# Windowed attention and Mish MLP: VectorE in written order up to the first product, and attention without GpSimd

## The chip, the core and the metric

The kernel runs on one core of a Trainium2 chip. The core has five engines, each with an instruction queue of its own that it works off in order: TensorE (PE, matrix products; its weight loads are listed apart as PEld), VectorE (DVE), ScalarE (ACT, table functions such as exp and Mish, and copies), GpSimd (POOL) and SyncE (SP, which issues the transfers). They wait for each other through semaphores. TensorE writes to PSUM, eight banks of 128 x 2 KB; VectorE and ScalarE read both PSUM and SBUF. The metric is the time of one execution in device microseconds; lower is better.

## The reference

A causal attention with a window of 128 and a linear bias, for 8 images of 8 heads, 576 positions and 64 columns, then a gated MLP over all 4608 rows of 512 columns with 2048 hidden units:

```python
def _attn_ref(q, k, v):
    scores = scale * np.matmul(q, k.transpose(0, 1, 3, 2))
    ...
    mask = (rel >= 0) & (rel < window)
    scores = np.where(mask, scores + bias[None], -1000000000.0)
    scores = scores - np.max(scores, axis=-1, keepdims=True)
    attn = np.exp(scores)
    attn = attn / (np.sum(attn, axis=-1, keepdims=True) + 1e-09)
    return np.matmul(attn, v).astype(np.float32)

def _moe_ref(x, w_in, w_out):
    h = x @ w_in
    sp = np.where(h > 20.0, h, np.log1p(np.exp(np.minimum(h, 20.0))))
    g = h * np.tanh(sp)
    return (g @ w_out).astype(np.float32)
```

The two weight matrices come in 64-bit floats.

## The kernel before

**Stages.** Per image c (0 to 7, the first 512 positions of each) there are three things: attention, a first product h = x w_in followed by Mish, and a second product by w_out. The 64 last positions of all images are put together as a ninth block. Attention of image 0 stands alone at the head. Attention of image c + 1 is written in between the steps of the second product of image c. Every float32 product is made of three products of high and low parts (float32r): x, the weights and g are each split into a rounded part and the rest.

**Attention.** `attention(b)` lists steps with a due number and sorts them. Heads go in pairs p = 0 to 3. A `unit(b, p, half)` is two blocks of 128 rows for both heads of a pair, so four blocks; `last_unit` does the last 64 rows of the pair. The steps of a unit: `scores` (TensorE into the tile s, two PSUM buffers), `exps` (a fused op on VectorE that scales, adds the bias and takes the row's minimum, then exp on ScalarE with the row's sum into sm), `fold` (adds the two halves of a 256-wide window block, since both use the same keys modulo the mask, and makes 1 / (sum + 1e-9)), `scale` (multiplies by it), `weights` (TensorE transposes, then one VectorE product with the two masks spreads the folded block into its two key blocks), `values` (TensorE, into o) and `split_x`. `last_unit` ends with a VectorE copy of its result into xo and a transfer of xo to memory (xs). xo has two buffers, so the copy of pair 2 uses that of pair 0. Before, `fold` adds on GpSimd (on VectorE in `last_unit`), and `scale` is a GpSimd op for image 0 and a VectorE op for the others.

**Weights.** `load_w` loads a piece of a weight in two halves (tiles wi0 to wi7, wo0 to wo7); all but the last piece, wo7, are issued on SyncE ahead of attention of image 0, and wo7 after the first product of image 0, into the tiles of x. `convert_w` turns a piece's 64-bit words into float32: in each half a ScalarE copy into a PSUM tile (ti or to, which takes the bank po0 or po1, or the bank w for wo7), three VectorE ops on 32-bit words that depend on each other, then a rounded copy on ScalarE and the rest on GpSimd, into si0 to si7 and so0 to so7. `convert_next` converts the next piece in the order wi0 to wi7, wo0 to wo7. Where it is called: at 3.6, 5.6 and 7.6 of image 0's attention (whose first unit starts at 0 and whose eighth at 7), then after each of the eight groups of the first product of image 0 once, from the fourth group on twice. The second product's tiles po0 and po1 take the same banks.

**What sets the order.** All engines' calls go through `InOrder`. TensorE and SyncE are kept in the written order. For the other three a scheduler places each instruction by a timeline that it estimates; it may move VectorE's ops of a conversion past those of attention. Every operation is recorded in line 30, so groups are told apart by their tiles: in the profile's names s, pz, sm, mx, o, x, h, g, gh, gl, po, ti, to, si, so; pz_0l to pz_3l and xo_0l to xo_3l belong to `last_unit` of pairs 0 to 3.

Of the kernel before, what the change touches and what calls it, by code (L numbers as in the profile page):

```python
# [8 lines left out]
F32 = mybir.dt.float32  # L9
# [3 lines left out]
AF = mybir.ActivationFunctionType  # L13
ALU = mybir.AluOpType

WINDOW = 128
P = 128
# [24 lines left out]
def attention_mish_mlp(  # L42
# [33 lines left out]
    at = ctx.enter_context(tc.tile_pool(name="at", bufs=2))  # L76
# [14 lines left out]
    for t in vb:  # L91
# [8 lines left out]
    pe, dve, act, pool, sp = engines = [  # L100
        InOrder(tc, e, e in (nc.tensor, nc.sync))
        for e in (nc.tensor, nc.vector, nc.scalar, nc.gpsimd, nc.sync)
    ]
# [126 lines left out]
    def unit(b, p, half):  # L230
# [6 lines left out]
        st = {}  # L237
        blocks = (0, 1) if half == 0 else (2, 3)
        name = f"{b}_{p}_{half}"
# [32 lines left out]
                )  # L272

        def fold():
            sm, pz = st["sm"], st["pz"]
            two = pz if half else pz[:, 1:4:2]
            pool.tensor_tensor(out=two[:, :, :P], in0=two[:, :, :P], in1=two[:, :, P:], op=ALU.add)
            dve.tensor_scalar(out=sm, in0=sm, scalar1=1e-9, scalar2=None, op0=ALU.add)
            dve.reciprocal(sm, sm)

        def scale():
            (pool if b == 0 else dve).tensor_tensor(
                out=st["pz"][:, :, :P], in0=st["pz"][:, :, :P],
                in1=st["sm"].rearrange("p (c n) -> p c n", n=1).to_broadcast([P, 4, P]), op=ALU.mult,
            )

        def weights():
            pz = st["pz"]
# [44 lines left out]
    def last_unit(b, p):  # L333

        st = {}
        name = f"{b}_{p}l"

        def scores():
            qk, z = qkv[(b, p)]

            st["s"] = qkv[("s", b, p)][:, :, :96]
            for i in range(2):
                pe.matmul(
                    st["s"][:, i, :], lhsT=z, rhs=qk[:, 1, 384 + 96 * i : 480 + 96 * i],
                    start=True, stop=True,
                )

        def exps():
            mx = at.tile([P, 1], F32, tag="mxl", name=f"mx{name}")
            sm = st["sm"] = at.tile([P, 1], F32, tag="sml", name=f"sm{name}")  # L350
            pz = st["pz"] = at.tile([P, 192], F32, tag="pzl", name=f"pz{name}")
            dve.tensor_tensor_reduce(
                out=pz.rearrange("p (a n) -> p a n", a=2), in0=st["s"],
                in1=nl[:, p, :].rearrange("p (a n) -> p a n", a=2), scale=-SCALE, scalar=3.0e38,
                op0=ALU.add, op1=ALU.min, accum_out=mx,
            )
            act.activation(pz, pz, AF.Exp, bias=mx, scale=-1.0, accum_out=sm)

        def fold():
            sm, pz = st["sm"], st["pz"]  # L360
            dve.tensor_scalar(out=sm, in0=sm, scalar1=1e-9, scalar2=None, op0=ALU.add)
            dve.reciprocal(sm, sm)
            dve.tensor_tensor(out=pz[:, :64], in0=pz[:, :64], in1=pz[:, P:], op=ALU.add)
            dve.tensor_scalar(out=pz[:, :P], in0=pz[:, :P], scalar1=sm, scalar2=None, op0=ALU.mult)

        def weights():
            t = st["t"] = ps.tile([P, 512], F32, tag="w", name=f"pt{name}")
            pe.transpose(t[:, :P], st["pz"][:, :P], ident)
            pf = st["pf"] = at.tile([P, 2, 2, 64], F32, tag="pfl", name=f"pf{name}", bufs=1)
            shape = [P, 2, 2, 64]  # L370
            dve.tensor_tensor(
                out=pf, in0=t[:, :P].rearrange("p (u i n) -> p u i n", u=1, i=2).to_broadcast(shape),
                in1=masks[:, :, :64].rearrange("p u (i n) -> p u i n", i=1).to_broadcast(shape),
                op=ALU.mult,
            )

        def values():
            va, vl = qkv[("v", b, p)]
            o = st["t"][:, P : P + LEFT]
            for n, val in enumerate((va[:, 3, :], vl)):  # L380
                for i in range(2):
                    pe.matmul(
                        o[HEAD[i]], lhsT=val[:, HEAD[i]], rhs=st["pf"][:, n, i, :],
                        start=(n == 0), stop=(n == 1), skip_group_check=True,
                    )
            xo = at.tile([P, LEFT], F32, tag="xo", name=f"xo{name}")
            dve.tensor_copy(xo, o)
            sp.dma_start(out=xs[p, :, b * LEFT : (b + 1) * LEFT], in_=xo)

        return [  # L390
            (0.01, scores), (0.5, exps), (0.9, fold), (1.4, weights), (1.995, values),
        ]

    def attention(b):

        steps = []
        for k in range(2 * NP):  # L400
            p, half = divmod(k, 2)
            for u in [unit(b, p, half)] + ([last_unit(b, p)] if half == 0 else []):
                steps += [(k + d, f) for d, f in u]
            if half:
                nxt = (b, p + 2) if p + 2 < NP else (b + 1, p + 2 - NP)
                if 0 < nxt[0] < B:
                    steps.append((k + 0.03, lambda nxt=nxt: load_pair(*nxt)))
                    steps.append((k + 2.01, lambda nxt=nxt: load_v(*nxt)))
        return sorted(steps, key=lambda s: s[0])
# [96 lines left out]
    def convert_next(tags=("po0", "po1")):  # L506
        if conv and conv[0] in raw_w:
            convert_w(*conv.pop(0), tags)

    early = [(k, lambda: convert_next()) for k in (3.6, 5.6, 7.6)]  # L510
    for _, work in sorted(attention(0) + early, key=lambda s: s[0]):
        work()

    for c in range(B + 1):
        for j in range(NJ):
            if c == 0:
                while ("i", j) not in split:
                    convert_next()
            if j == NJ - 1:
                parts(c, 0, 0)  # L520
                parts(c, 0, 1)
            first(c, j)
            if c == 0:
                for _ in range(2 if j > 2 else 1):
                    convert_next()
        if c == 0:
            load_w(*last_w)

        n = 4 * NJ
        steps = []  # L530
        for m in range(2 * NJ):
            for t in range(2):
                steps.append((2 * m + t, lambda m=m, t=t: second(c, *divmod(m, NJ), t)))
            if m >= 2:
                steps.append((2 * m - 4.1, lambda m=m: parts(c, *divmod(m, NJ))))
            if c == 0:
                steps.append((2 * m + 0.5, lambda: convert_next(("w", "w"))))
        if c + 1 < B:
            steps += [((n - 2) / 9.0 * s - 0.2, f) for s, f in attention(c + 1)]
        elif c + 1 == B:  # L540
            steps.append((4.5, last_x))
        for _, work in sorted(steps, key=lambda s: s[0]):
            work()
# [63 lines left out]
```

## Time and profile before

| | us |
|---|---|
| median of three runs | 1056.3 (1055.12 to 1056.61) |
| the profiled execution | 1056.28 |
| its span, first to last instruction | 1054.5 |
| first product of image 0 starts on TensorE | 88.03 |
| second product of image 0 starts | 134.78 |
| first product of image 1 starts | 208.3 |

The profile shows one execution. Section 1 of its page has the busy time of each engine; section 2 cuts the span into 40 slices, with tenths of busy time and the clock that TensorE was granted; the chain of work that ended last is followed back from the end:

```profile
PE 85%; DMA 4%; DVE 4%; issue 3%; POOL 2%; ACT 1%; SPq 0%; POOLq 0%; DVEq 0%
```

In rows of a timeline the columns are start, duration, engine, line, operation, out<-in, sizes and count (of equal instructions merged), and in brackets the idle time before it on its engine and what ended it.

### The profile page before, as it was taken

How to read it: one execution, taken by the hardware profiler on the slowest of the kernel's cores; microseconds unless marked ns; L12 is line 12 of the kernel's file. 1: busy time of each engine (PE TensorE's matmuls, PEld its weight loads, DVE VectorE, ACT ScalarE, POOL GpSimd, SP SyncE). 2: the span in 40 equal slices, each digit the busy share in tenths (PEclk: the TensorE clock that was granted, in tenths of full speed). 3: DMA queues.
4: the chain of work that ended last, by engine and by line, in shares of the span. 5: the costliest groups of instructions: out<-in, count | busy, mean ns of one | idle time of the engine just before them, and what ended most of it. 6: DMA issues, size and time to landing. Idle time of an engine off the chain costs nothing.

```text
span 1054.5 us, 14241 instructions
## 1 busy us (share of the span) xinstructions
PE 998.6 (95%) x5280; PEld 787.4 (75%) x5280; DVE 405.7 (38%) x1166; ACT 391.5 (37%) x926; POOL 309.7 (29%) x270
## 2 busy tenths in 40 slices
PE   4548989999999999999999999999999999999998
PEld 2336867787778877887778777877787778888886
DVE  4998067502760167106630564037501760000000
ACT  2544554323433345215422443235323442222221
POOL 3513754211431044004410342123311441041032
PEclk9567989999999999999999999999999999999999
DMA  8940022200220023002120032002100201000001
GB/s 269 399 159 13 1 66 91 70 1 20 64 71 32 1 62 93 33 1 60 58 68 1 25 93 68 1 24 85 58 21 1 71 25 41 20 21 21 1 1 40
DMA packets 52133, 59.32 MB, mean 56 GB/s; under 512 B 13024, under 2 KB 32608, under 8 KB 52064
## 3 DMA queue, kind: packets, MB, share of 16 engines
q1 hardware_dynamic: 50880, 57.69, 17.1%
q8 instruction: 42, 0.69, 0.3%
q10 hardware_dynamic: 1184, 0.72, 0.2%
q14 instruction: 27, 0.22, 0.1%
HBM read 47.91 MB, written 10.49 MB: 55 GB/s over the span
## 4 chain that ended last, share of the span: by engine, by line
PE 85%; DMA 4%; DVE 4%; issue 3%; POOL 2%; ACT 1%; SPq 0%; POOLq 0%; DVEq 0%
PE po L30 38%; PE h L30 33%; PE s L30 9%; PE o L30 5%; DMA wi<-in_moe_w_in_dram 2%; DMA wo<-in_moe_w_out_dram 1%; DVE pz L30 1%; POOL si L30 1%; DVE ti L30 1%; POOL so L30 1%; DVE to L30 1%; DMA nb<-in_relb_dram 1%; DVE wi L30 0%; SPq L30 0%; DMA first<-in_k_dram 0%
## 5 line engine op out<-in xcount | busy, mean ns | idle before, releaser
L30 PE MATMUL h<-x,si 128*128 128x512 f32 x1728 | 394.9, 390 | 0.0
L30 PEld LDWEIGHTS h<-x,si 128*128 128x128 f32 x1728 | 325.5, 188 | 68.0 <-issue 0.3
L30 PE MATMUL po<-so,gh 128*128 128x512 f32 x1152 | 324.8, 404 | 0.0
L30 POOL TENSOR_TENSOR gl<-g,gh 128x512 fp32r<-128x512 f32 x144 | 193.6, 1344 | 376.5 <-ACT gh L30 347.0
L30 PEld LDWEIGHTS po<-so,gh 128*128 128x128 f32 x1152 | 207.5, 189 | 48.6 <-ACT x L30 7.0
L30 DVE CUSTOM_DVE_ANT_0 pz<-s,nb 128x256 f32<-128x256 f32 (+1 forms) x256 | 84.6, 386 | 345.6 <-PE s L30 336.0
L30 PE MATMUL po<-so,gl 128*128 128x512 f32 x576 | 178.7, 391 | 0.0
L30 ACT ACTIVATE g<-h 128x1024 f32<-128x1024 f32 x72 | 74.0, 1028 | 268.8 <-PE h L30 268.8
L30 ACT ACTIVATE pz<-pz,mx 128x256 f32<-128x256 f32 (+1 forms) x256 | 120.3, 471 | 118.0 <-DVE mx L30 117.9
L30 POOL TENSOR_TENSOR pz<-pz 128x256 f32<-128x256 f32 x64 | 64.8, 1013 | 314.9 <-PE po L30 174.0
L30 ACT ACTIVATE gh<-g 128x512 fp32r<-128x512 f32 x144 | 90.6, 629 | 116.6 <-PE po L30 112.4
L30 PEld LDWEIGHTS po<-so,gl 128*128 128x128 f32 x576 | 108.6, 188 | 24.2
L30 DVE TENSOR_TENSOR pz<-s,masks 128x1024 f32<-128x1024 f32 x64 | 78.2, 1222 | 29.2 <-PE s L30 29.2
L30 DVE TENSOR_TENSOR pz<-pz,sm 128x512 f32<-128x512 f32 x56 | 61.9, 1106 | 11.0 <-POOL pz L30 8.9
L30 DVE COPY ob<-po 128x512 f32<-128x512 f32 x18 | 12.4, 692 | 124.9 <-PE po L30 124.9
L30 PE MATMUL s<-qk 64*128 64x128 f32 (+1 forms) x448 | 57.7, 376 | 0.0
L30 PE MATMUL o<-pz,va 128*64 128x128 f32 (+1 forms) x560 | 54.9, 325 | 0.0
L30 PEld LDWEIGHTS o<-pz,va 128*64 128x64 f32 x560 | 33.3, 136 | 27.8 <-issue 10.2
L30 ACT ACTIVATE x<-o 128x512 fp32r<-128x512 f32 x32 | 19.1, 598 | 83.8 <-PE o L30 83.8
L30 PE MATMUL o<-pz,first 128*64 128x128 f32 (+1 forms) x80 | 14.1, 517 | 36.0 <-DVE pz L30 36.0
L30 PE MATMUL s<-ident,pz 128*128 128x128 f32 x256 | 41.1, 286 | 7.4 <-POOL pz L30 4.3
L30 ACT ACTIVATION_READ_ACCUMULATOR pz<-pz,mx 128x1 f32 x256 | 47.8, 187 | 0.0
(114 smaller groups left out, 556.9 us busy)
## 6 DMA issues: line engine op xcount, KB each, us to landing
wi<-in_moe_w_in_dram SPq DMA_DIRECT2D x16, 512.0 KB, 10.4
wo<-in_moe_w_out_dram SPq DMA_DIRECT2D x16, 512.0 KB, 10.8
out_dram<-ob SPq DMA_DIRECT2D x32, 256.0 KB, 2.0
qk<-in_q_dram SPq DMA_DIRECT2D x28, 288.0 KB, 3.7
qk<-in_k_dram SPq DMA_DIRECT2D x28, 288.0 KB, 3.7
va<-in_v_dram SPq DMA_DIRECT2D x28, 256.0 KB, 2.9
first<-in_q_dram SPq DMA_DIRECT2D x4, 288.0 KB, 3.9
first<-in_k_dram SPq DMA_DIRECT2D x4, 288.0 KB, 4.4
```

Source lines behind the costliest of these rows:

```text
L30: ins = method(*args, **kwargs)
```

## The change

VectorE's wrapper is switched to the written order (`dve.fixed = True`) from the head of image 0's attention until the load of wo7 behind its first product. Of the three conversions in that attention the one at 7.6 stays, and each group of the first product is now followed by two. In attention of all images, GpSimd's addition goes: for the blocks that are 256 wide, one fused VectorE op per block adds the two halves and multiplies by the reciprocal (its minimum output `un` is not read); the two blocks that are 128 wide (in units with half 0) are scaled on ScalarE, and the addition of 1e-9 moves from VectorE to ScalarE.

```diff
         def fold():
+            sm = st["sm"]
+            act.activation(sm, sm, AF.Copy, bias=1e-9)
+            dve.reciprocal(sm, sm)
+
+        def scale():
+
             sm, pz = st["sm"], st["pz"]
-            two = pz if half else pz[:, 1:4:2]
-            pool.tensor_tensor(out=two[:, :, :P], in0=two[:, :, :P], in1=two[:, :, P:], op=ALU.add)
-            dve.tensor_scalar(out=sm, in0=sm, scalar1=1e-9, scalar2=None, op0=ALU.add)
-            dve.reciprocal(sm, sm)
-
-        def scale():
-            (pool if b == 0 else dve).tensor_tensor(
-                out=st["pz"][:, :, :P], in0=st["pz"][:, :, :P],
-                in1=st["sm"].rearrange("p (c n) -> p c n", n=1).to_broadcast([P, 4, P]), op=ALU.mult,
-            )
+            unread = at.tile([P, 4], F32, tag="un", name=f"un{name}")
+            for c in range(4):
+                if half or c % 2:
+                    dve.tensor_tensor_reduce(
+                        out=pz[:, c, :P], in0=pz[:, c, :P], in1=pz[:, c, P:], scale=sm[:, c : c + 1],
+                        scalar=3.0e38, op0=ALU.add, op1=ALU.min, accum_out=unread[:, c : c + 1],
+                    )
+                else:
+                    act.activation(pz[:, c, :P], pz[:, c, :P], AF.Copy, scale=sm[:, c : c + 1])
...
         def fold():
             sm, pz = st["sm"], st["pz"]
-            dve.tensor_scalar(out=sm, in0=sm, scalar1=1e-9, scalar2=None, op0=ALU.add)
+            act.activation(sm, sm, AF.Copy, bias=1e-9)
             dve.reciprocal(sm, sm)
-            dve.tensor_tensor(out=pz[:, :64], in0=pz[:, :64], in1=pz[:, P:], op=ALU.add)
-            dve.tensor_scalar(out=pz[:, :P], in0=pz[:, :P], scalar1=sm, scalar2=None, op0=ALU.mult)
+            un = at.tile([P, 1], F32, tag="unl", name=f"un{name}")
+            dve.tensor_tensor_reduce(
+                out=pz[:, :64], in0=pz[:, :64], in1=pz[:, P:], scale=sm, scalar=3.0e38,
+                op0=ALU.add, op1=ALU.min, accum_out=un,
+            )
+            act.activation(pz[:, 64:P], pz[:, 64:P], AF.Copy, scale=sm)
...
-    early = [(k, lambda: convert_next()) for k in (3.6, 5.6, 7.6)]
-    for _, work in sorted(attention(0) + early, key=lambda s: s[0]):
+
+    dve.fixed = True
+    for _, work in sorted(attention(0) + [(7.6, convert_next)], key=lambda s: s[0]):
         work()
...
             if c == 0:
-                for _ in range(2 if j > 2 else 1):
+                for _ in range(2):
                     convert_next()
         if c == 0:
             load_w(*last_w)
+            dve.fixed = False
```

What this does to the engines' queues is seen at three places. In the names the first figure is the image (or the weight's number for ti, to, si, so, wi, wo), and the last one a buffer. The first place is VectorE around the copy of xo for pair 2 of image 0. Before:

```order
L30 COPY xo0_2l_458<-pt0_2l_426 128x64
L30 TENSOR_SCALAR ti7_1_761<-ti7_1_761 128x512
L30 TENSOR_SCALAR to0_0_796<-to0_0_796 128x512
L30 SCALAR_TENSOR_TENSOR ti7_1_761<-wi7_158,ti7_1_761 128x512
L30 ISA pz0_3_0_470,mx0_3_0_468<-s0_3_0_461,nb_76 128x128
```

After:

```order
L30 RECIPROCAL sm0_2_1_409<-sm0_2_1_409 128x4
L30 ISA pz0_2_1_410,un0_2_1_435<-pz0_2_1_410,sm0_2_1_409 128x128
L30 COPY xo0_2l_449<-pt0_2l_429 128x64
L30 ISA pz0_3_0_461,mx0_3_0_459<-s0_3_0_452,nb_76 128x128
L30 TENSOR_TENSOR pz0_2_1_410<-s0_2_1_400,masks_91 128x2x4x128
```

Before, words of wi7 and wo0 stand around the copy (those of wi0 to wi6 are ahead of it); after, no conversion is ahead of it, and pair 3's first softmax op follows directly. The second place is ScalarE around the first Mish of image 0 (g, with the table load ahead of it). Before:

```order
L30 ACTIVATE to4_1_916<-wo4_173 128x512
L30 ACTIVATE to5_0_924<-wo5_176 128x512
L30 ACT_TABLE_LOAD
L30 ACTIVATE g0_0_612<-h0_0_587 128x1024
L30 ACTIVATE si3_614<-wi3_146 128x512 x2
L30 ACTIVATE si4_655<-wi4_149 128x512 x2
```

After:

```order
L30 ACTIVATE x0_3_582<-o0_3_556 128x512
L30 ACTIVATE ti2_0_628<-wi2_143 128x512
L30 ACTIVATE ti2_1_635<-wi2_143 128x512
L30 ACT_TABLE_LOAD
L30 ACTIVATE g0_0_610<-h0_0_585 128x1024
L30 ACTIVATE si1_612<-wi1_140 128x512 x2
L30 ACTIVATE gh0_0_0_981<-g0_0_610 128x512
L30 ACTIVATE si2_627<-wi2_143 128x512
```

The rounded copies behind the first Mish were those of pieces 3 and 4; now they are those of pieces 1 and 2. In the second form the instruction that waits for h (a wait of its own, not shown as a row) stands ahead of the table load; before it is the Mish itself that waits. The third place is ScalarE at the end of the first product of image 0. Before:

```order
L30 ACTIVATE so3_866<-wo3_170 128x512 x2
L30 ACTIVATE g0_3_906<-h0_6_881 128x1024
L30 ACTIVATE so4_908<-wo4_173 128x512 x2
L30 ACTIVATE so5_923<-wo5_176 128x512 x2
L30 ACTIVATE g0_3_906<-h0_7_946 128x1024
L30 ACTIVATE to7_0_1017<-wo7_0_987 128x512
L30 ACT_TABLE_LOAD
```

After:

```order
L30 ACTIVATE to4_0_910<-wo4_173 128x512
L30 ACTIVATE to7_0_1045<-wo7_0_1015 128x512
L30 ACTIVATE so3_894<-wo3_170 128x512
L30 ACTIVATE to4_1_917<-wo4_173 128x512
L30 ACTIVATE so4_909<-wo4_173 128x512
L30 ACTIVATE g0_3_949<-h0_6_924 128x1024
L30 ACTIVATE to5_0_952<-wo5_176 128x512
L30 ACTIVATE g0_3_949<-h0_7_989 128x1024
L30 ACTIVATE to7_1_1052<-wo7_1_1016 128x512
```

The copy of wo7's first half, which waits for that piece's load, stood behind the last Mish; now it stands ahead of the last two, and the copies of wo4 and wo5 stand between them.

More of the change, by code (lines that the diff above doesn't have):

```diff
@@ L274, in fold @@
         def fold():
-            sm, pz = st["sm"], st["pz"]
-            two = pz if half else pz[:, 1:4:2]
-            pool.tensor_tensor(out=two[:, :, :P], in0=two[:, :, :P], in1=two[:, :, P:], op=ALU.add)
-            dve.tensor_scalar(out=sm, in0=sm, scalar1=1e-9, scalar2=None, op0=ALU.add)
+            sm = st["sm"]
+            act.activation(sm, sm, AF.Copy, bias=1e-9)
             dve.reciprocal(sm, sm)
         def scale():
-            (pool if b == 0 else dve).tensor_tensor(
-                out=st["pz"][:, :, :P], in0=st["pz"][:, :, :P],
-                in1=st["sm"].rearrange("p (c n) -> p c n", n=1).to_broadcast([P, 4, P]), op=ALU.mult,
-            )
+            sm, pz = st["sm"], st["pz"]
+            unread = at.tile([P, 4], F32, tag="un", name=f"un{name}")
[7 more added lines that the diff above has]
+                    act.activation(pz[:, c, :P], pz[:, c, :P], AF.Copy, scale=sm[:, c : c + 1])
         def weights():
```

## The prediction

> **What bounds the kernel now.** First the page: busy times and the clock in its 40 slices; then the span cut into five stages at events of the timeline.
>
> ```profile
> PE 998.6 (95%) x5280; PEld 787.4 (75%) x5280; DVE 405.7 (38%) x1166; ACT 391.5 (37%) x926; POOL 309.7 (29%) x270
> PEclk9567989999999999999999999999999999999999
> ```
>
> TensorE is busy 95% of the span, and after the first six slices its clock is granted in full. The stages (columns: stretch, its length, then busy time and count of each engine, granted clock, DMA share, GB/s):
>
> ```profile
> 0.00:88.03 88.03, 40.96 (x229) 27.42 (x229) 72.20 (x194) 38.90 (x107) 27.69 (x44) 0.71 0.73 252
> 88.03:133.45 45.42, 45.42 (x194) 37.20 (x192) 13.08 (x22) 25.79 (x39) 29.54 (x24) 0.96 0.00 1
> 133.45:153.60 20.15, 15.88 (x68) 11.65 (x68) 14.72 (x36) 11.99 (x30) 13.66 (x11) 0.83 0.25 84
> 153.60:208.30 54.70, 54.70 (x354) 41.83 (x354) 35.09 (x105) 22.13 (x69) 19.59 (x16) 1.00 0.23 69
> 208.30:1054.50 846.20, 841.64 (x4441) 669.33 (x4439) 270.56 (x812) 292.70 (x682) 219.23 (x176) 1.00 0.12 37
> ```
>
> Until 88.03 it is VectorE (72.20 of 88.03) that works on the first image's attention and on the weights' words. The first product of image 0 then runs without a gap to 133.45. Between 133.45 and 153.60 TensorE lacks 4.27 us; from 153.60, the first attention-times-values of image 1, it never waits (its busy time fills the stretches up to a few records missing from the trace). So only the head of the kernel can give or lose time. TensorE's order of work is the same after the change, so the result is set by when it reaches that same instruction.
>
> **The change, step 1: when the first product starts.** VectorE now does the attention in written order, with one weight converted in it instead of what the scheduler slipped in. That takes more than 30 us of conversion off VectorE before the product, so attention runs faster at first; no transfer is moved. But written order also makes the copy of xo for pair 2 stand ahead of pair 3's work, and that copy reuses the buffer of pair 0 (two buffers), which a store to memory must have read:
>
> ```profile
> 9.60 0.29 DVE L30 CUSTOM_DVE_ANT_0 pz<-s,nb 128x128 f32<-128x128 f32 x1 [9.60 <-DMA first<-in_k_dram]
> 9.82 0.29 DVE L30 CUSTOM_DVE_ANT_0 pz<-s,nb 128x128 f32<-128x128 f32 x1
> 16.37 1.55 PE L30 MATMUL o<-pz,first 128*64 128x256 f32 x8 [1.26 <-DVE pz L30]
> 51.99 0.33 SPq L30 DMA_DIRECT2D xs<-xo_0l  x1
> xs<-xo_0l SPq DMA_DIRECT2D x1, 32.0 KB, 9.1
> 64.60 0.21 DVE L30 COPY xo_2l<-pt_2l 128x64 f32<-128x64 f32 x1
> ```
>
> The store is issued at 51.99, behind the last weight load on SyncE, and lands 9.1 us later, at 61.1, since seven weight loads are queued before it. SyncE's order and those loads don't change, so it lands at 61.1 again. Before, the copy ran at 64.60 and waited for nothing. After, VectorE gets there in the forties: in the one unit that no weight disturbed it read the first scores at 9.60 and the values product ran at 16.37, 6.8 us later, and five units and a half at 6.5 to 6.8 make 36 on top of 9.6. So VectorE stands for about 14 us with everything of pair 3 queued behind the copy. What is left from 61.1, by the rows of the same work before:
>
> ```profile
> 67.05 0.42 DVE L30 CUSTOM_DVE_ANT_0 pz<-s,nb 128x256 f32<-128x256 f32 x1
> 67.39 0.42 DVE L30 CUSTOM_DVE_ANT_0 pz<-s,nb 128x256 f32<-128x256 f32 x1
> 68.61 1.22 DVE L30 TENSOR_TENSOR pz<-s,masks 128x1024 f32<-128x1024 f32 x1
> 69.88 1.98 PE L30 MATMUL o<-pz,first 128*64 128x128 f32 x12 [4.87 <-DVE pz L30]
> 71.79 2.08 PE L30 MATMUL s<-first 64*128 64x256 f32 x8
> 83.02 1.11 PE L30 MATMUL s<-ident,pz 128*128 128x128 f32 x4 [2.09 <-POOL pz L30]
> 99.28 1.30 DVE L30 TENSOR_SCALAR to<-to 128x512 uint32<-128x512 uint32 x2 [3.80 <-ACT to L30]
> 103.18 0.70 DVE L30 TENSOR_SCALAR to<-to 128x512 uint32<-128x512 uint32 x1 [0.23 <-ACT to L30]
> 103.91 0.70 DVE L30 SCALAR_TENSOR_TENSOR to<-wo,to 128x512 uint32<-128x512 uint32 x1
> 104.64 0.69 DVE L30 SCALAR_TENSOR_TENSOR wo<-wo,to 128x512 uint32<-128x512 uint32 x1
> 88.03 45.49 PE L30 MATMUL h<-x,si 128*128 128x512 f32 x192
> 208.46 43.52 PE h L30 x192
> ```
>
> Scores of 3_0 and the mask of 2_1 to 63.5 (two softmax ops 0.21 apart, two 0.34 apart, then the mask, 1.1); values and the next scores on TensorE, 1.9 + 2.1, to 67.8; four softmax ops at 0.34, a mask and the small one, to 70.7; then the one early weight. Its three ops in a half depend on each other and start 0.73 apart where nothing is put between them (103.18 to 104.64), while two that don't depend take 1.30 together, 0.6 apart. So a half takes 0.73 + 0.73 + 0.6, about 2.05, and a weight 4.1, to 74.8, and the unit's reciprocal stands behind it. Reciprocal and four fused ops (0.21 apart, as the 128-wide softmax op) to 75.7; then transposes, mask and values, which from 83.02 to 88.03 took 5.0 with about 1 of other VectorE work between: **the first product starts at 79.7**, 8.3 earlier than 88.03. ScalarE's new small ops, of 1 to 128 columns, have no row: they cost more than nothing and less than the 0.58 of a 512-wide copy below (2.31 for four); I take 0.2 to 0.3. At five of eight units they lie in the 14 us of standing and cost nothing; for the rest both ends together move the sum by under 0.5. GpSimd's additions and scalings go, for units before the copy in the same shadow.
>
> **Step 2: the first product itself.** Before, weights 0 to 2 were ready at its start; after, weight 0 alone is. Weight 1's copy on ScalarE stands behind the table load and the first Mish (the rows of the change above), and the Mish's wait for TensorE now stands ahead of the table load, which before ran while the product did.
>
> ```profile
> 92.35 1.28 ACT L30 ACT_TABLE_LOAD   x1
> 95.48 1.03 ACT L30 ACTIVATE g<-h 128x1024 f32<-128x1024 f32 x1 [1.85 <-PE h L30]
> 96.40 2.31 ACT L30 ACTIVATE si<-wi 128x512 fp32r<-128x512 f32 x4
> 97.13 5.14 POOL L30 TENSOR_TENSOR si<-wi,si 128x512 fp32r<-128x512 f32 x4 [14.16 <-ACT si L30]
> ```
>
> A group of 24 products takes 43.52 / 8 = 5.44 at full clock; the first product of before lost 45.49 - 43.52 = 2.0 to the half clock at its start, and I give group 0 the 1.1 that falls into it, so it ends at 86.3. Then 1.28 table, 0.92 Mish, 0.6 copy: TensorE waits 2.8 us, gets the high part at 89.1, and the low halves from GpSimd at 90.4 and 91.6 (5.14 for four). With the clock back at half, group 1 ends near 97.8, where an undisturbed one would end at 91.7: **6.1 lost**. Later groups need 5.44 each and a weight comes every 4.1 to 4.5, so they follow without gaps: the product ends at 97.8 + 6 x 5.44 = 130.5, only 3 us ahead of 133.45.
>
> **Step 3: after it.** The second product's first tile takes the same PSUM bank (po0) that the conversions use. Before, VectorE was through with them at 105.3 (104.64 + 0.69). After, 14 weights are left when the last split ends, two 512-wide ops of 0.6 behind the last values: 81.1. To the last half in that bank stand 27 halves at 2.03, 54.8; six ops of the last weight at 0.6, 3.6; softmax of image 1's first unit with its reciprocals and fused ops, 2.4; and waits for ScalarE, which is in order too. Those: behind the first Mish 2.0, behind the second one, late with group 1, 2.6, and 1.6 in which ScalarE stands for the last weight's load, with about 1.3 in small ones. That load's wait now stands ahead of copies and of two Mish:
>
> ```profile
> 136.38 0.62 ACT L30 ACTIVATE to<-wo 128x512 f32<-128x512 f32 x1 [1.65 <-DMA wo<-in_moe_w_out_dram]
> 132.94 0.95 SPq L30 DMA_DIRECT2D wo<-in_moe_w_out_dram  x2
> 146.26 1.09 PE L30 MATMUL s<-ident,pz 128*128 128x128 f32 x4 [3.12 <-DVE pz L30]
> 148.50 0.45 PE L30 MATMUL pt_0l<-ident,pz_0l 128*128 128x128 f32 x1 [1.14 <-DVE wo L30]
> 134.78 1.18 PE L30 MATMUL po<-so,gh 128*128 128x512 f32 x4
> ```
>
> The sum is 149.4, less some 0.9 where two weights interleave: **the second product starts at 148.5**, against 134.78. On the way TensorE stands twice: for the Mish of the last groups, some 8 us to 138.3, before it may write image 1's scores, then 7.5 for the bank. From the second product's start to the first values of image 1 before took 18.82, of which 4.26 waits (the two quoted) and about 2.6 half clock (0.83 granted over 20.15 is 6.9 at half, some 5.2 of them busy), so 11.9 of work; after, with 1.7 of half clock, 13.6: 162.1 instead of 153.60. **So 8.5 us later.**
>
> **What may block the fused ops.** They read two operands from SBUF. The nearest rows, the addition of 64 columns alone and under a GpSimd op:
>
> ```profile
> 29.66 0.21 DVE L30 TENSOR_TENSOR pz_1l<-pz_1l 128x64 f32<-128x64 f32 x1
> 142.36 0.74 POOL L30 TENSOR_TENSOR pz<-pz 128x256 f32<-128x256 f32 x1
> 142.59 0.59 DVE L30 TENSOR_TENSOR pz_0l<-pz_0l 128x64 f32<-128x64 f32 x1
> ```
>
> At 142.59 it ended just behind GpSimd's op, 0.38 late. A fused op may be like it, or free like the softmax op, which reads PSUM and one SBUF tile. Two places have GpSimd busy on the path, the scale of 3_1 at 75 and that of image 1's first unit at 147: 0 to 2 x 1.3 us, perhaps 4 with the clock windows missed. I take one, 1.3, as the addition is the nearer row. The Trainium skill, page "SBUF — State Buffer", section "Who interferes with whom", says that a VectorE instruction with two SBUF inputs contends with a GpSimd instruction that reads SBUF; by that rule both are blocked and the time would be 1069, without it 1065. The row at 142.59 agrees for the addition; no row has the fused op.
>
> **Steady part.** From image 1 on an attention unit has slack:
>
> ```profile
> 165.82 1.29 POOL L30 TENSOR_TENSOR pz<-pz 128x512 f32<-128x512 f32 x1 [3.41 <-ACT pz L30]
> 167.58 1.34 DVE L30 TENSOR_TENSOR pz<-pz,sm 128x512 f32<-128x512 f32 x1
> 172.91 0.60 PE L30 MATMUL s<-ident,pz 128*128 128x128 f32 x4
> ```
>
> The last exponential ends before 165.82 and the transposes come at 172.91. After: 0.3 + 0.1 + four fused ops, 0.85, or four times 1.3 if each is blocked: 171.4 at worst, still in time. I cost the seven later images at nothing; without that cover each unit would add what it is late.
>
> **The sum.** The profiled execution took 1056.28 (span 1054.5 and 1.78 around it), the median is 1056.3. 1056.3 + 8.5 + 1.3 = **1066**.
>
> **Rivals.** (a) VectorE's words keep ahead, faster than before: ops at 0.6 throughout, as in the interleaved pieces, and no wait for ScalarE give 84 x 0.6 = 50.4 us from 81.1, so the bank is free at 131.5, about when the first product ends. Then only steps 1 and 2 count, and the 4.3 us of waits before go too: 1056.3 - 8.3 + 6.1 - 4.3 = 1050. It decides at one point, whether weight words end before TensorE is through group 7. Against it: dependent ops do start 0.73 apart in the one stretch without neighbours. 0.07. (b) The copy doesn't stand, because the store lands soon after its issue: the product starts some 8 us earlier, the words too, and the bank is free at 141: about 1057, no change. Against it is the 9.1. With other partial reliefs 0.08. (c) Blocking bites at both places and at later units: 1069 to 1074, 0.15. (d) My forecast, 1060 to 1069: 0.70.
>
> A difference of 0.2%, 2.1 us, is about what a measurement of this kernel can tell from no change. Faster by more: (a), 0.07. Within: (b), 0.08. Slower: 0.85. The range that holds 8 in 10 runs from 1059 to 1072: its low end has half of step 3's waits gone, its high end both blocks and one more clock window at half.
>
> **What would show it.** Right: VectorE idle from about 46 to 61.1 ahead of the xo copy of pair 2; first product at 79 to 81; a gap of 3 us before its second group with the table load behind the first; first second-product at 148 to 152, waiting for VectorE; the first values of image 1 at 161 to 166; no TensorE idle later. Wrong: no idle ahead of the copy; a second product before 140; TensorE gaps that repeat in each image.

## The result, and the profile after

The changed kernel takes 1067.47 us (median of 4 runs, 1065.71 to 1069.18) beside 1056.23 us for the kernel before (4 runs, 1055.12 to 1056.61): a ratio of 1.0108, 95% interval 1.009 to 1.0126. Timed once more in a later comparison it was 1067.89 beside 1055.91, 1.0118 (1.0103 to 1.0134). It is slower by 11 to 12 us, about 1.1%.

| us | before | after |
|---|---|---|
| the profiled execution | 1056.28 | 1065.71 |
| its span | 1054.5 | 1064.0 |
| first product of image 0, start to end | 88.03 to 133.45 | 80.25 to 130.49 |
| second product of image 0 starts | 134.78 | 149.93 |
| first values of image 1 | 153.60 | 163.06 |
| from there to the end of the span | 900.9 | 900.94 |

The last row says where to look: behind the first values of image 1 the two executions are alike to 0.1 us, so the 9.5 us by which the spans differ arise ahead of them. The medians lie 11.2 us apart: the profiled execution of the changed kernel is the shortest of its four, and e9 below shows where 1.3 us of the rest arise. First the page of the changed kernel, busy times and the clock in 40 slices:

```profile
PE 997.9 (94%) x5280; PEld 786.3 (74%) x5280; DVE 401.8 (38%) x1398; ACT 431.6 (41%) x1118; POOL 233.4 (22%) x198
PEclk9659969999999999999999999999999999999999
```

TensorE's busy time is that of before. GpSimd lost 76 us of work, and ScalarE gained 40; by the last row of the table above, that changes nothing behind the first values of image 1. Then the stages (stretch, its length, busy time and count of PE, PEld, DVE, ACT and POOL, granted clock, DMA share, GB/s):

```profile
0.00:80.25 80.25, 39.09 (x229) 25.88 (x229) 39.34 (x165) 29.77 (x106) 6.51 (x24) 0.73 0.79 276
80.25:130.49 50.24, 46.60 (x194) 37.42 (x192) 43.38 (x65) 32.86 (x52) 29.77 (x23) 0.95 0.00 1
130.49:149.93 19.44, 2.75 (x13) 1.86 (x13) 18.01 (x43) 14.24 (x32) 7.76 (x6) 0.56 0.15 54
149.93:163.06 13.13, 13.13 (x56) 10.04 (x56) 6.06 (x15) 6.63 (x16) 8.71 (x7) 0.88 0.16 49
```

VectorE's work of the head moved and did not shrink: up to the first product it has 39 us instead of 72, during that product 43 instead of 13. In the third stretch, from the end of the first product to the start of the second, TensorE works 2.75 of 19.44 us. Before, that stretch took 1.33 us (133.45 to 134.78), so it is 18.1 longer; 3.0 of them come back because the first product ends earlier, and 5.7 because the stretch behind it takes 13.13 us instead of 18.82. What VectorE does in it, and why it is late, is in its timeline (the row with SPq is SyncE's issue of the store, and the row under it the time from this issue to its landing):

```profile
46.01 0.08 DVE L30 DVE_READ_ACCUMULATOR2_ANT un<- 128x1 f32 x1
51.34 0.33 SPq L30 DMA_DIRECT2D xs<-xo_0l  x1
xs<-xo_0l SPq DMA_DIRECT2D x1, 32.0 KB, 9.1
60.49 0.23 DVE L30 COPY xo_2l<-pt_2l 128x64 f32<-128x64 f32 x1 [14.40 <-DMA xs<-xo_0l]
74.77 0.35 DVE L30 CUSTOM_DVE_ANT_0 pz<-pz,sm 128x128 f32<-128x128 f32 x1
75.04 1.38 DVE L30 CUSTOM_DVE_ANT_0 pz<-pz,sm 128x128 f32<-128x128 f32 x1
147.44 1.35 DVE L30 CUSTOM_DVE_ANT_0 pz<-pz,sm 128x128 f32<-128x128 f32 x1
149.20 0.68 DVE L30 SCALAR_TENSOR_TENSOR wo<-wo,to 128x512 uint32<-128x512 uint32 x1
```

VectorE stands 14.40 us ahead of the copy of pair 2, released by the store of xo for pair 0. That store is issued at 51.34 and lands 9.1 us later, at 60.4; over all eight images the same store takes 2.2 us in the median, and between 40 and 54 us, with the weight loads in flight, the DMA queues move 410 GB/s. Later two fused ops take 1.38 and 1.35 us where the one beside them takes 0.35. The op at 149.20 is the last word in bank po0; it ends at 149.88. TensorE's timeline has the other half, with ScalarE's table load between the first two groups:

```profile
80.25 6.32 PE L30 MATMUL h<-x,si 128*128 128x512 f32 x24
86.64 1.28 ACT L30 ACT_TABLE_LOAD   x1 [0.17 <-PE h L30]
89.55 0.73 PE L30 MATMUL h<-x,si 128*128 128x512 f32 x2 [2.99 <-ACT si L30]
138.29 1.65 PE L30 MATMUL s<-qk 64*128 64x128 f32 x8 [7.80 <-ACT g L30]
149.93 2.07 PE L30 MATMUL po<-so,gh 128*128 128x512 f32 x4 [8.89 <-DVE wo L30]
163.06 0.87 PE L30 MATMUL o<-pz,va 128*64 128x256 f32 x8
```

It waits 2.99 us for weight 1, 7.80 us for the Mish of the last groups, and 8.89 us for VectorE's words, until 0.05 us after the op above ended.

### The profile page after: what moved, and what is told of

It reads as the page before. It is cut to its first block, busy times and chain, and to the rows that moved or that the text cites. A ratio compares the mean times of both kernels' runs of the same rounds, so it can differ in the third digit from the quotient of the medians.

```text
span 1064.0 us, 14440 instructions
## 1 busy us (share of the span) xinstructions
PE 997.9 (94%) x5280; PEld 786.3 (74%) x5280; DVE 401.8 (38%) x1398; ACT 431.6 (41%) x1118; POOL 233.4 (22%) x198
## 4 chain that ended last, share of the span: by engine, by line
PE 90%; DMA 5%; DVE 3%; issue 1%; SPq 1%; ACT 0%; POOL 0%; POOLq 0%; DVEq 0%
PE po L30 38%; PE h L30 36%; PE s L30 9%; PE o L30 5%; DMA wi<-in_moe_w_in_dram 2%; DMA wo<-in_moe_w_out_dram 1%; DVE pz L30 1%; DMA xs<-xo_0l 1%; SPq L30 1%; DVE to L30 1%; DMA nb<-in_relb_dram 1%; DMA first<-in_k_dram 0%; DVE ti L30 0%; DVE wo L30 0%; PE pt_1l L30 0%
## 5 line engine op out<-in xcount | busy, mean ns | idle before, releaser
L30 POOL TENSOR_TENSOR gl<-g,gh 128x512 fp32r<-128x512 f32 x144 | 188.1, 1307 | 711.8 <-ACT gh L30 684.0
L30 DVE CUSTOM_DVE_ANT_0 pz<-pz,sm 128x128 f32<-128x128 f32 x192 | 87.2, 500 | 1.3
L30 PEld LDWEIGHTS s<-qk 64*128 64x128 f32 x448 | 34.3, 188 | 19.1 <-ACT g L30 8.2
L30 PEld LDWEIGHTS s<-ident,pz 128*128 128x128 f32 x256 | 33.1, 146 | 18.6 <-issue 5.9
```

Source lines behind the costliest of these rows:

```text
L30: ins = method(*args, **kwargs)
```

## The experiments

Every run was timed beside the kernel before; ratios are to it. Each edit is against the changed kernel, except where the text says otherwise.

| run | us | ratio (95%) |
|---|---|---|
| changed kernel, second time (e9) | 1067.89 | 1.0118 (1.0103 to 1.0134) |
| e1 four xo buffers | 1051.68 | 0.9967 (0.9956 to 0.9979) |
| e2 attention edit alone | 1054.62 | 0.9991 (0.9982 to 0.9999) |
| e3 written order alone | 1064.73 | 1.0085 (1.0073 to 1.0097) |
| e10 written order alone, four xo buffers | 1050.91 | 0.9954 (0.9941 to 0.9967) |
| e11 kernel before, four xo buffers | 1055.79 | 1.0000 (0.9991 to 1.0009) |
| e4 other banks for the words | 1065.07 | 1.0092 (1.0079 to 1.0105) |
| e5 three weights in the standing | 1048.25 | 0.9931 (0.9919 to 0.9943) |
| e7 two GpSimd reads away | 1065.54 | 1.0094 (1.0081 to 1.0107) |
| e8 table loaded early | 1067.51 | 1.0102 (1.0089 to 1.0115) |
| e6 combined | 1040.68 | 0.9864 (0.9851 to 0.9877) |
| e12 combined, attention as before | 1041.48 | 0.9870 (0.9852 to 0.9887) |

**The changed kernel again (e9).** No edit.

> The changed kernel itself, timed once more beside the two below, since runs of these kernels spread by 3 to 5 us. All theories: 1065 to 1069, ratio to the kernel before 1.009 to 1.013.

It came out as in the first comparison, so the other runs can be set against either. Its profiled execution took 1067.05 us, 1.34 more than that of the first comparison, and VectorE's timeline says why:

```profile
61.76 0.23 DVE L30 COPY xo_2l<-pt_2l 128x64 f32<-128x64 f32 x1 [15.60 <-DMA xs<-xo_0l]
```

SyncE issued the store at 52.59 instead of 51.34, the copy ran 1.27 us later, and everything behind it is shifted by the same: the first product starts at 81.50, the second at 151.20, the first values of image 1 at 164.40. So the difference between these two executions is the landing of this store, and profiles of kernels that stand for it are best compared counted from the copy.

**The standing ahead of the xo copy (e1).**

```diff
-            xo = at.tile([P, LEFT], F32, tag="xo", name=f"xo{name}")
+            xo = at.tile([P, LEFT], F32, tag="xo", name=f"xo{name}", bufs=4)
```

> The changed kernel with four buffers for xo instead of two, so that the copy of pair 2's last unit waits for no store. Nothing else is changed. Theory (the 14.4 us for which VectorE stands ahead of that copy are the price of the written order, and all that follows moves with it): the copy runs at about 47 instead of 60.5, the first product starts at 68 to 70 instead of 80.25, the second at 136 to 139 instead of 149.93, and the time is 1053 to 1056, 12 to 14 us less than the changed kernel and as fast as or faster than the kernel before. First rival (the prediction's case b): the earlier start is partly eaten by the words, which still have to be converted; the product starts 8 us earlier and the time is near 1057. Second rival (the words of the 14 remaining weights alone set the second product, whenever the first one starts): the product starts at 69, but the second stays at 147 to 150 and the time at 1065 to 1067.

The time falls by 15 us, from slower than before to faster than before. VectorE's timeline in this run:

```profile
47.06 0.23 DVE L30 COPY xo_2l<-pt_2l 128x64 f32<-128x64 f32 x1 [0.45 <-PE pt_2l L30]
```

And TensorE's:

```profile
69.34 6.84 PE L30 MATMUL h<-x,si 128*128 128x512 f32 x24
79.19 1.22 PE L30 MATMUL h<-x,si 128*128 128x512 f32 x2 [3.00 <-ACT si L30]
137.66 2.07 PE L30 MATMUL po<-so,gh 128*128 128x512 f32 x4 [9.09 <-DVE wo L30]
151.92 0.87 PE L30 MATMUL o<-pz,va 128*64 128x256 f32 x8
```

The copy runs 13.4 us earlier, the first product 10.9, the second 12.3, the first values of image 1 11.1. The waits ahead of the second group and of the second product, 3.00 and 9.09, are as they were, and that for the Mish of the last groups is 5.09 instead of 7.80: the whole chain moved. So the standing is what makes the change a loss, and neither rival of this run holds. The profiled execution of this run took 1054.56, as the theory had it; it was the longest of ten (1049.61 to 1054.56), and the median lies 1.3 below the range expected.

**The two parts apart (e2, e3).** e2 puts the new `fold` and `scale` into the kernel before; e3 takes them out of the changed kernel.

> The kernel before with the attention edit alone: GpSimd's addition and scaling replaced by the fused ops and ScalarE's scaled copies; the scheduler still orders VectorE and all three early conversions stay. Theory (the edit shortens the chain of each unit of image 0, since GpSimd's addition of 1.3 us and its scaling go, and costs nothing in the later images because the units there have slack): the first product starts 2 to 3 us earlier than 88.03, the time is 1052 to 1054. Rival (the fused ops are blocked by GpSimd in many places and the two small ops on ScalarE lengthen the chain): the first product starts at 88 to 90 and the time is 1056 to 1059.

> The changed kernel with attention as it was before: only VectorE's written order up to the first product and the moved conversions are left. Theory (the written order is what costs; it does so by the standing ahead of the xo copy and by the weights that are not ready): VectorE idle to about 61 ahead of the copy, first product at 80 to 81, second at 147 to 150, time 1062 to 1066. Rival (the two parts add up: whatever the attention edit alone brings against the kernel before is what this kernel lacks against the changed one): the time is the changed kernel's 1067.5 plus what the attention edit saves alone, so 1070 to 1072 if that saves 3 to 4 us. Second rival (attention costs the loss): near 1056.

The attention edit alone is a small gain, 0.9991: less than the theory's 2 to 4 us, but no loss, so its rival falls as well. In its profile TensorE's rows read:

```profile
85.96 45.78 PE L30 MATMUL h<-x,si 128*128 128x512 f32 x192
146.73 0.45 PE L30 MATMUL pt_0l<-ident,pz_0l 128*128 128x128 f32 x1 [2.93 <-DVE wo L30]
151.97 0.87 PE L30 MATMUL o<-pz,va 128*64 128x256 f32 x8
```

The first product starts 2.1 us earlier, of which 1.6 reach image 1; a wait for the last weight's words, 1.14 us before, is now 2.93. The written order alone is the loss, 1.0085, and it shows the same standing, in VectorE's timeline of e3:

```profile
61.24 0.23 DVE L30 COPY xo_2l<-pt_2l 128x64 f32<-128x64 f32 x1 [16.34 <-DMA xs<-xo_0l]
```

The two ratios give 1.0076 when multiplied; both together measured 1.0108 and 1.0118. So the parts do not seem to just add up: on top of the written order the attention edit costs some 3 us (the interval of e3 overlaps that of the first comparison and is clear of that of e9). The first rival of e3 (1070 to 1072) had the sign of that the wrong way. Two candidates for these 3 us are the blocked fused ops and the table load (e7, e8 below): with the old attention, TensorE's gap ahead of the second group was 1.68 us and not 2.99. The profiled executions do not place them further: e3's was the longest of its five and the changed kernel's the shortest of its four, and the first values of image 1 come at 163.23 and 163.06. Counted from the xo copy, the second product starts 4.0 us earlier in e3, but the first values of image 1 only 0.6.

**Where the buffers bind (e10, e11).** The edit of e1, once in e3 and once in the kernel before.

> Only the written order and the moved conversions, attention as before, and four buffers for xo. Theory (without the standing the written order is a gain by itself, and the attention edit adds nothing to it because its two blocked fused ops and the table load behind the wait cost about what GpSimd's addition did): first product at 68 to 70, time 1048 to 1052, the same as with the attention edit (1051.7) or up to 3 us less. Rival (the attention edit is worth here what it was worth alone): 1052.5 to 1055, 1 to 3 us more than with it.

> The kernel before with four buffers for xo and nothing else. Theory (the store's landing binds only where the written order puts the copy early; in the kernel before, the copy of pair 2 ran at 64.60, after the landing at 61.1): no change, within 0.2% of the kernel before, first product at 87 to 89. Rival (the two buffers held the scheduler's order back too, unseen): the first product starts 3 us or more earlier and the time falls to 1050 to 1053.

In the kernel before, four buffers do nothing (ratio 1.0000): its copy ran after the store had landed in any case, and the rival falls. With the written order they take 14 us off e3. The attention edit, which costs some 3 us with two buffers, makes no measurable difference with four (0.9967 with it, 0.9954 without, intervals that overlap); whether its cost depends on the buffers at all is not shown, since 0.13% and 0.23 to 0.33% are too close for these intervals. The written order with its moved conversions, once the copy does not stand, is 0.5% faster than the kernel before.

**The bank of the words (e4).**

```diff
                 for _ in range(2):
-                    convert_next()
+                    convert_next(("w", "o"))
```

> The changed kernel with the conversions behind the groups of the first product put into the PSUM banks w and o instead of po0 and po1, so that no conversion holds a bank of the second product. Theory as the prediction put it (the held bank po0 is what delays the second product, and so image 1): the 8.89 us wait for VectorE ahead of the second product is gone, it starts at 139 to 142 instead of 149.93, the first values of image 1 come 8 to 10 us earlier and the time is 1057 to 1060. Rival (the bank only carries the wait; VectorE's words stand ahead of image 1's reciprocals and fused ops, so the queue is the bound): the second product starts at 139 to 142, but TensorE then waits for VectorE 5 to 8 us ahead of image 1's transposes or values, and the time is 1063 to 1066, only 2 to 4 us less than the changed kernel.

TensorE's timeline in this run:

```profile
139.98 1.64 PE L30 MATMUL po<-so,gh 128*128 128x512 f32 x4
157.59 0.45 PE L30 MATMUL pt_0l<-ident,pz_0l 128*128 128x128 f32 x1 [7.33 <-DVE wo L30]
162.37 0.87 PE L30 MATMUL o<-pz,va 128*64 128x256 f32 x8
```

And VectorE's:

```profile
151.00 0.08 DVE L30 DVE_READ_ACCUMULATOR2_ANT un_0l<- 128x1 f32 x1
156.75 0.69 DVE L30 SCALAR_TENSOR_TENSOR wo<-wo,to 128x512 uint32<-128x512 uint32 x1
```

The second product starts right behind image 1's first scores, 9.95 us earlier: the bank was the cause of the 8.89. But the time comes down by only 2 to 3 us (the intervals of the changed kernel and of this run still overlap), as the rival had it. TensorE now waits 7.33 us at the transposes of image 1's last unit. What they read was ready at 151.08 (the fused op behind `un_0l`); they go only when the word at 156.75 has ended, at 157.44. Those transposes write to bank w, which the last weight's words hold in both kernels. So the wait moved from one held bank to the next, and the rival's time is right but its reason is not shown: it named the order of VectorE's queue. Whether that order alone would hold image 1 back, were no bank held, wasn't tried.

**Words in the standing (e5).**

```diff
-    for _, work in sorted(attention(0) + [(7.6, convert_next)], key=lambda s: s[0]):
+    for _, work in sorted(attention(0) + [(5.99, lambda: convert_next())] * 3, key=lambda s: s[0]):
```

> The changed kernel (two xo buffers) with three weights converted directly ahead of pair 2's last values and xo copy, instead of one at the end of image 0's attention. VectorE so has 3 x 4.1 = 12.3 us of words to do in the 14.4 us for which it stood. Theory (the standing is free time on VectorE that only lacks work written ahead of it; what the words of later weights cost is time after the first product): the copy still runs at 60 to 61, the first product starts at 76, four us earlier than 80.25 as no words are left behind the copy, the 3 us gap ahead of its second group is gone, the second product starts 17 to 20 us earlier (130 to 133), and the time is 1047 to 1051. Rival (the words held the attention up elsewhere, or ScalarE's and GpSimd's share of them lands on the chain of pair 3): the first product stays at 80 or later, and the time is 1058 to 1064: the gap and one weight are saved, no more.

VectorE's timeline around the copy:

```profile
46.32 0.69 DVE L30 TENSOR_SCALAR ti<-ti 128x512 uint32<-128x512 uint32 x1
58.09 0.69 DVE L30 SCALAR_TENSOR_TENSOR wi<-wi,ti 128x512 uint32<-128x512 uint32 x1
61.60 0.23 DVE L30 COPY xo_2l<-pt_2l 128x64 f32<-128x64 f32 x1 [2.82 <-DMA xs<-xo_0l]
```

And TensorE's:

```profile
75.17 32.93 PE L30 MATMUL h<-x,si 128*128 128x512 f32 x144
111.00 11.17 PE L30 MATMUL h<-x,si 128*128 128x512 f32 x48 [2.90 <-ACT g L30]
127.76 1.66 PE L30 MATMUL s<-qk 64*128 64x128 f32 x8 [5.59 <-ACT g L30]
130.22 2.05 PE L30 MATMUL po<-so,gh 128*128 128x512 f32 x4
143.26 0.87 PE L30 MATMUL o<-pz,va 128*64 128x256 f32 x8
```

The copy waits for the same store and runs 1.1 us later than it did, as the store was issued 1.1 later (52.42), but 18 word ops (46.32 to 58.78) fill the time before it. Six groups run without a gap from 75.17, and the second product waits for no word; what is left are two waits for a Mish, 2.90 and 5.59. That is 19 us better than the changed kernel, with the buffers unchanged and the copy no earlier, and 3 to 4 us better than e1, which took the wait away. So the 14.4 us were lost not because VectorE waited, but because nothing was written ahead of the wait.

**The blocked fused ops (e7).** The second halves of weight 0 of w_in and weight 5 of w_out get a low part of zero.

```diff
-            pool.tensor_tensor(out=low, in0=val, in1=up.bitcast(F32), op=ALU.subtract)
+            if (kind, j, a) in (("i", 0, 1), ("o", 5, 1)):
+                pool.memset(low.bitcast(F32), 0.0)
+            else:
+                pool.tensor_tensor(out=low, in0=val, in1=up.bitcast(F32), op=ALU.subtract)
```

> The changed kernel with two of GpSimd's 32 subtractions for the weights' low parts replaced by a memset to zero (the second half of weight 0 of w_in and of weight 5 of w_out): the low part of these two halves is left out of the products. They are the two GpSimd ops under which a fused op took 1.38 and 1.35 us instead of 0.35. Theory (a fused op that starts under a GpSimd op with SBUF operands stands until that ends): both fused ops take 0.35, the first product starts 1 us earlier, the second one 2 us earlier, time 1064.5 to 1066.5, 1 to 3 us less than the changed kernel. Rival (the long fused ops are not on the path, because VectorE waits elsewhere between them and the second product): time as the changed kernel's, 1067 to 1068. Second rival (a memset that only writes blocks them too): the fused ops stay above 0.6 us.

In the changed kernel the two subtractions stand in GpSimd's timeline at:

```profile
74.87 1.40 POOL L30 TENSOR_TENSOR si<-wi,si 128x512 fp32r<-128x512 f32 x1 [0.77 <-ACT si L30]
147.35 1.29 POOL L30 TENSOR_TENSOR so<-wo,so 128x512 fp32r<-128x512 f32 x1 [3.11 <-ACT so L30]
```

They end at 76.27 and 148.64, and the fused ops, which started 0.17 and 0.09 us behind them, end 0.15 us later. The same two fused ops in VectorE's timeline of this run, the fourth of its unit and the first of image 1's:

```profile
75.84 0.35 DVE L30 CUSTOM_DVE_ANT_0 pz<-pz,sm 128x128 f32<-128x128 f32 x1
147.66 0.35 DVE L30 CUSTOM_DVE_ANT_0 pz<-pz,sm 128x128 f32<-128x128 f32 x1
```

Both take 0.35 us: the reading GpSimd op was what held them. The median is about 2 us lower (1.0094 against 1.0118 and 1.0108), which fits 1.03 + 1.00 us saved, though the intervals still overlap. The trace puts it on the path: counted from the xo copy, which ran at 61.29 here, the first product starts 1.04 us earlier than in the changed kernel, the second 1.58 and the first values of image 1 1.70. The memsets ran at other times than the fused ops, so whether an op that only writes would block is left open.

**The table load (e8).**

```diff
+    warm = const.tile([P, 1], F32, tag="warm", name="warm")
+    pool.memset(warm, 0.0)
+    act.activation(warm, warm, AF.Mish)
```

> The changed kernel with a Mish of one column of a zeroed tile written behind image 0's attention, so that ScalarE's table is loaded before it waits for the first group's h. Theory (the load of 1.28 us stands between the end of h and the Mish only because of where the wait is): TensorE's gap ahead of the second group is 1.7 us instead of 2.99, and since ScalarE's copies for the next weights come 1.3 us earlier too, the second product follows: time 1065.5 to 1067, 1 to 2 us less. Rival (VectorE's words set the second product, and they don't wait for that Mish): the gap shrinks, the second product stays at 149 to 150, time 1067 to 1068, no change.

TensorE's timeline:

```profile
88.62 0.73 PE L30 MATMUL h<-x,si 128*128 128x512 f32 x2 [1.66 <-ACT si L30]
147.51 2.07 PE L30 MATMUL po<-so,gh 128*128 128x512 f32 x4 [8.89 <-DVE wo L30]
```

and the stretch from there to the first values of image 1:

```profile
147.51:162.01 14.50, 14.49 (x55) 10.97 (x55) 6.06 (x15) 6.65 (x16) 8.70 (x7) 0.79 0.15 45
```

The gap shrank by 1.33 us, and the second product started 2.4 us earlier (2.8 counted from the xo copy), against the rival; the time, 1067.51, does not tell the two apart (1.0102, interval 1.0089 to 1.0115). In the profiled execution part of the gain went where no theory had put it: the next stretch took 14.50 us instead of 13.13, at a granted clock of 0.79 instead of 0.88. Counted from the copy, 1.4 us are left at the first values of image 1. Whether the time falls by 1 to 2 us or not at all stays open.

**All together (e6, e12).** Four xo buffers, the banks of e4, and two weights at 5.99 in place of the one at 7.6; e12 is the same with attention as before.

> The changed kernel with four buffers for xo, two weights converted ahead of pair 2's last values (none at the end of image 0's attention), and the later conversions in the PSUM banks w and o. Theory (standing, late weights and the held bank were the three losses, and what is left is 12 weights' words behind the first product's start): first product at 68 to 70, no wait of 3 us ahead of its second group, second product at 122 to 125, first values of image 1 at 136 to 139, time 1040 to 1045, less than both kernels. Rival (as in the run with other banks alone, the words queue ahead of image 1's first ops and eat what the banks give): TensorE waits 5 us or more ahead of image 1's transposes, time 1046 to 1051.

> The combined kernel (four xo buffers, two weights ahead of pair 2's last values, banks w and o) with attention as it was before. Theory (the attention edit is worth about nothing where VectorE is in written order; the gain comes from where the words stand): time 1039 to 1043, as the combined kernel's 1040.7 within 0.2%. Rival (the combined kernel needs the freed GpSimd and the shorter chain of a unit): 2 to 5 us more, 1043 to 1046.

TensorE's timeline of the combined kernel:

```profile
67.52 32.95 PE L30 MATMUL h<-x,si 128*128 128x512 f32 x144
102.81 12.76 PE L30 MATMUL h<-x,si 128*128 128x512 f32 x48 [2.34 <-ACT g L30]
121.77 1.87 PE L30 MATMUL po<-so,gh 128*128 128x512 f32 x4
133.27 0.30 PE L30 MATMUL pt_0l<-ident,pz_0l 128*128 128x128 f32 x1 [1.98 <-DVE wo L30]
137.84 0.87 PE L30 MATMUL o<-pz,va 128*64 128x256 f32 x8
```

It beats the kernel before by 1.4% and the changed one by 2.4 to 2.5%. The wait for the words at image 1's transposes is 1.98 us here and not 7.33 as in e4, with 13 weights and the last one left behind the first product's start instead of 14 and the last (the expectation above counted 12 in all); that this is the whole reason is not shown. The old attention gives the same (0.9870), so the gain lies in the buffers, the banks and where VectorE's words stand; how it is shared among the three was not taken apart here.

## Why the prediction was right, step by step

The forecast was 1066.0 with a range of 1059 to 1072; 1067.47 and 1067.89 were measured. Between the profiled executions the forecast was 8.5 + 1.3 = 9.8 us and came out as 9.43.

- **Step 1, right.** The standing was forecast at 14 us to 61.1 and measured 14.40 to 60.49, with the store landing 9.1 us after its issue as it did before. First product: 79.7 forecast, 80.25 measured, with 1.03 lost on the way at the fused op of 75.04 that the prediction counted apart. e1 and e11 show that the cause is this store and the two buffers, and e9 that the end moves with the landing.
- **Step 2, right.** Gap 2.8, measured 2.99; second group at 89.1, measured 89.55; end of the product 130.5, measured 130.49. That the end fits to 0.01 is luck: the product started 0.55 later than forecast and took 50.24 us where 50.8 were forecast. The table load behind the wait is 1.28 us of the gap; e8 takes 1.33 off it.
- **Step 3, right in place and size, incomplete in reason.** Waits of 8 and 7.5 us were forecast, 7.80 and 8.89 measured; the second product was forecast at 148.5, with the blocked op apart, and came at 149.93. The waits of VectorE for ScalarE on the way were taken at 7.5 us and add up to 6.0. The prediction gave the held bank po0 as the reason. e4 confirms the bank for that wait, and shows that freeing it alone saves only 2 to 3 us, since the last weight's words then hold bank w. Both banks are late for the same work, the 14 weights and the last one still to convert behind the first product's start: an earlier start alone leaves the wait at 9.09 us (e1), while with 12 and the last one left there is no wait for words (e5).
- **The fused ops, half counted.** Two places were named and one was taken, at 1.3 us. Both were blocked, at 1.03 and 1.00 (1.38 and 1.35 less 0.35), so this term of the sum is 2.03, and rival (c) had that half right: later units are held too, but their time does not show at the end, and the median stayed below its 1069. By the rule of the Trainium skill (page "SBUF — State Buffer", section "Who interferes with whom") both were to be blocked; the trace and e7 agree with it, for a fused op too. The estimate of 0.21 us from one fused op to the next was low: 74.77 to 75.04 is 0.27.
- **Steady part, right.** 900.94 us from the first values of image 1 on, against 900.9.
- **Rival (b), mispriced.** It had about 1057 if the copy did not stand. e1 gives 1051.68. What it had too small is the move: 8 us at the first product, where 10.9 were measured, and the bank free at 141, where the second product started at 137.66 (12.3 earlier), because the wait for the Mish of the last groups shrank as well, from 7.80 to 5.09.
- **Rival (a), words ahead throughout:** not seen in the changed kernel. e5 comes to what it looked for, with no wait for words and 1048.25 beside 1050; since that is by another arrangement, the closeness is chance.
- **Not priced:** that the attention edit by itself gains a little (0.9991), and costs some 3 us on top of the written order with two buffers; where these 3 us arise stays open beyond the two candidates of e7 and e8.

## What to carry to other kernels

When an engine is put into written order, look in that order for every instruction that waits for something slow, however small it is: here a copy of 64 columns that waits for a 32 KB store behind bulk loads cost 14 to 16 us of the end time (e3 against e10, the changed kernel against e1). Either give its buffer enough copies or write independent work ahead of it, and count the work that is pushed behind the next engine's start, because that is where it comes back as a wait. A PSUM bank held by late work was a symptom here: with it free, the time was 2 to 3 us lower and the wait turned up at the next bank; it went when less work was left behind.

## What was not expected of the hardware

The fused ops stand under GpSimd in the later images as well, where it costs nothing. The group's row on the page of the changed kernel:

```profile
L30 DVE CUSTOM_DVE_ANT_0 pz<-pz,sm 128x128 f32<-128x128 f32 x192 | 87.2, 500 | 1.3
```

The busy time of 87.2 counts overlapping ops once; the mean of 500 ns times 192 is 96.0 us, where 0.35 each would be 67.2. In the timeline 162 of them take 0.35 and 30 take 1.17 to 1.44. Each of these 30 ends 0.14 to 0.16 us behind the end of a GpSimd subtraction beside which it ran, and no fused op that started under one took 0.35. The other way round, in 38 places a GpSimd subtraction starts while a fused op runs, and that op keeps its 0.35. A softmax op, which reads PSUM and one SBUF tile, was not held when it started under one: 18 with 256 columns took 0.42, as the others did. A place in image 1 shows the order of starting at its sharpest, VectorE first:

```profile
184.55 0.35 DVE L30 CUSTOM_DVE_ANT_0 pz<-pz,sm 128x128 f32<-128x128 f32 x1
184.82 1.37 DVE L30 CUSTOM_DVE_ANT_0 pz<-pz,sm 128x128 f32<-128x128 f32 x1
```

and GpSimd:

```profile
184.67 1.37 POOL L30 TENSOR_TENSOR gl<-g,gh 128x512 fp32r<-128x512 f32 x1 [4.47 <-ACT gh L30]
```

The op that starts 0.12 us ahead of GpSimd's is not touched; the one that starts 0.15 us behind it ends 0.15 us after it, at 186.19 against 186.04.

Executions of one kernel spread more than expected of differences of 1 to 2 us: e1's ten lie between 1049.61 and 1054.56, and roughly go with the clock that TensorE was granted (1054.56 at a mean of 0.964, 1050.30 at 0.981). The kernel before shows no such order in the same comparison (1053.90 at 0.969, 1055.59 at 0.980), and in the changed kernel 1.3 us of the spread are the landing of the store (e9). A single profile can so lie 3 us off its kernel's median, as e1's did.
